# Expert activations made transposed, with the gates spread over the rank rows by a trip through DRAM

## The chip, the core and the metric

The kernel runs on one core of a Trainium2 chip. The metric is the device time of one execution in microseconds; before the change it is 426.72 us, the median of three runs (426.12 to 431.16).

## What is computed

An attention with spatially reduced keys, followed by a mixture of adapters. For each of 4 batches, 12288 queries of 128 channels attend to 768 keys, which are 4x4 means of `kv` times `w_sr` (keys and values are the same). Each of the 49152 results `x` is then routed to its best two of 8 experts, each a product of rank 16, and the gated sum is added to `x`:

```python
kv_pool = kv.reshape(B, H//4, 4, W//4, 4, C).mean(axis=(2, 4))
k = v = kv_pool.reshape(B, -1, C) @ w_sr
a = softmax(q @ k.T / sqrt(C));  x = (a @ v).reshape(B*N, C)
logits = x @ w_gate                      # 8 experts
w = softmax over the two largest logits  # 0 for the other six
out = x + sum_e w[:, e] * ((x @ A[e]) @ B[e])   # A: 128x16, B: 16x128
```

## The kernel before

The queries are cut into 96 chunks of 512 tokens (four sub-blocks `s` of 128). One round of the main loop (a step, loop variable `k`) issues the scores of chunk `k` and, woven between them by hand, the later stages of earlier chunks. Nearly everything keeps the order in which it is written (`keep`), on every engine's queue. The stages of one chunk:

- `scores` (L237): three pairs of matmuls `sg` (512 columns each) and three exponentials `em` on ScalarE. `sg` has two buffers in PSUM.
- `attend` (L247): 24 matmuls `acc`, six first and eighteen at the end of the step; one buffer in PSUM. `normalize` (L255): `rinv` and `xn` on VectorE, which also makes the logits of the experts.
- `top`, `route`, `gates` (L275 to L315): four `srt` on VectorE; then the gates of a whole group on GpSimd with a tanh on ScalarE. Groups have 1, 1, 2, then eighteen times 4, eight times 2 and four times 1 chunks (L268); `first` and `size` name them. The tensor `gw` holds the gates with tokens on the partitions.
- `transposes` (L317): four TensorE transposes of `xn` of one chunk, and in the same PSUM tile `tt_ps` four of `hg` of the chunk before it; one copy `tts` of both on VectorE (on ScalarE in the tail, the steps from 96 on, when there is nothing left to score).
- `down` (L341): four matmuls `h_ps`, with a sub-block of `xT` as weights and `a_bf` moving; the result has tokens on the partitions and expert and rank along the row. `gate` (L346): one VectorE multiplication of `h_ps` by `gw`, broadcast over the rank, gives `hg`.
- `up` (L355): four matmuls `d_ps` with a sub-block of `hgT` as weights. `finish` (L360): one VectorE addition `osb`, one store to `out` from the SP queue.

All PSUM tiles but `sg` and `acc` (that is `tt_ps`, `h_ps`, `d_ps`, and those of the key preparation) take turns in the two buffers of one pool (`mtile`, L70): a tile has to wait until the one but one before it has been read.

Which step a chunk enters at (its `transposes` of `xn` and its `down`) is counted out ahead in `enter` (L409 to L416): one step after its group is normalized (`late`), one chunk per step, in a few steps two (`two`). A chunk of a group of four enters six steps after its scores; the last chunk enters at step 97, and the loop ends two steps later.

The SP queue issues, in program order, the loads of `kv` for the next batch (two of 256 KB per step in steps 4 to 15 of each 24), every fourth step a transposing load `qT` (L84) of 512 KB made from a bf16 copy of `q`, which GpSimd's queue has cast from DRAM to DRAM (`cast_q`, L77), and the store of each chunk. GpSimd also adds up the `kv` rows of the next batch (L169) between the gates.

Of the kernel before, what the change touches and what calls it, by code (L numbers as in the profile page):

```python
# [11 lines left out]
BF16 = mybir.dt.bfloat16  # L12
U16 = mybir.dt.uint16
FP16 = mybir.dt.float16
AF = mybir.ActivationFunctionType
ALU = mybir.AluOpType
# [4 lines left out]
def kernel(  # L21
# [10 lines left out]
    nc = tc.nc  # L32
    P = 128
    B, N, C = q.tensor.shape
    E, RK = 8, 16
# [3 lines left out]
    T = 512  # L39
    S = T // P  # L40
    GC = 4
    GT = GC * T
# [7 lines left out]
    prep = ctx.enter_context(tc.tile_pool(name="prep", bufs=1))  # L50
    kvpool = ctx.enter_context(tc.tile_pool(name="kvpool", bufs=3))
    per_b = ctx.enter_context(tc.tile_pool(name="per_b", bufs=2))
    qpool = ctx.enter_context(tc.tile_pool(name="qpool", bufs=4))
    ppool = ctx.enter_context(tc.tile_pool(name="ppool", bufs=7))
    xpool = ctx.enter_context(tc.tile_pool(name="xpool", bufs=5))
    rpool = ctx.enter_context(tc.tile_pool(name="rpool", bufs=4))
    gpool = ctx.enter_context(tc.tile_pool(name="gpool", bufs=6))
    run = ctx.enter_context(tc.tile_pool(name="run", bufs=3))
    opool = ctx.enter_context(tc.tile_pool(name="opool", bufs=6))
    qdram = ctx.enter_context(tc.tile_pool(name="qdram", bufs=1, space=bass.MemoryType.DRAM))  # L60
    ps_s = ctx.enter_context(tc.tile_pool(name="ps_s", bufs=2, space=bass.MemoryType.PSUM))
    ps_a = ctx.enter_context(tc.tile_pool(name="ps_a", bufs=1, space=bass.MemoryType.PSUM))
# [4 lines left out]
    def mm(*a, **k):  # L67
        return keep(nc.tensor.matmul(*a, **k))  # L68

    def mtile(shape, dtype=FP32, name="mb"):  # L70
        return ps_m.tile(shape, dtype, tag="mb", name=name)
# [55 lines left out]
    for m in range(GC):  # L127
        load_q(1, m * S, m * S + S)
    b_f = const.tile([P, C], FP32)
    keep(nc.sync.dma_start(b_f, moe_B.rearrange("e r c -> (e r) c")))  # L130
    a_f = const.tile([P, P], FP32)
    keep(nc.sync.dma_start(a_f, moe_A.rearrange("e c r -> c e r")))

# [5 lines left out]
    make_identity(nc, id_f)  # L139
    id_bf = const.tile([P, P], BF16)  # L140
    nc.vector.tensor_copy(id_bf, id_f)
    wext = const.tile([P, VC], FP32)
    nc.vector.tensor_copy(wext[:, 0:C], w_sr_sb)
    wT_ps = mtile([P, C], name="wT_ps")
# [86 lines left out]


    em, acc, xn, xg, srt, gw = {}, {}, {}, {}, {}, {}
    tts, xT, hgT, hp, hg, dp = {}, {}, {}, {}, {}, {}
    R = J // 2

    def scores(k, r):  # L237
# [41 lines left out]
        for s in range(S):  # L279
            keep(nc.vector.max(srt[k0][:, m, s], xn[k][:, s, C:VC]))  # L280

    later = []

    def route(k0):
        n = size[k0] * S
# [23 lines left out]
    def gates(k0, n, eng, arg, mask):  # L309
        th = rpool.tile([P, GC * S, 8], FP32, tag="th", name="th")[:, 0:n]  # L310
        keep(nc.scalar.activation(th, arg, AF.Tanh, bias=0.0, scale=0.5))  # L311
        w = gpool.tile([P, GC * S, 8], FP32, tag="gw", name="gw")
        keep(eng.tensor_tensor(w[:, 0:n], th, mask, op=ALU.mult))  # L313
        keep(eng.tensor_tensor(w[:, 0:n], w[:, 0:n], mask, op=ALU.add))  # L314
        gw[k0] = w  # L315

    def transposes(kx, kh, tail):  # L317

# [21 lines left out]

    def down(k):  # L341
        hp[k] = mtile([P, S, P], name="h_ps")
        for s in range(S):
            mm(hp[k][:, s], xT[k][:, s], a_bf, start=(s == 0), stop=(s == S - 1))

    def gate(k):  # L346
        k0, m = first[k], k - first[k]
        hg[k] = run.tile([P, S, P], BF16, tag="hg", name="hg")
        keep(nc.vector.tensor_tensor(  # L349
            hg[k].rearrange("p s (e r) -> p (s e) r", e=E),  # L350
            hp[k].rearrange("p s (e r) -> p (s e) r", e=E),
            gw[k0][:, m * S:(m + 1) * S].rearrange("p s e -> p (s e)")
            .unsqueeze(2).broadcast_to([P, S * E, RK]), op=ALU.mult))

    def up(k):  # L355
        dp[k] = mtile([P, S, C], name="d_ps")
# [10 lines left out]
            d.pop(k, None)  # L367

    LA = 4

    for m in range(GC):
        turn_q(0, m, nc.scalar)
# [20 lines left out]
    for g in range(2, 4):  # L393
        cast_q(g)
    a_bf = const.tile([P, P], BF16)
    keep(nc.vector.tensor_scalar(a_bf, a_f, 0.5, None, op0=ALU.mult))
    b_bf = const.tile([P, C], BF16)
    keep(nc.vector.tensor_copy(b_bf, b_f))
    turn_q(1, 0, nc.scalar)
# [10 lines left out]
    e = 0  # L410
    for k in range(NCHUNK):
        done = normed[first[k] + size[k] - 1]
        late = k < NCHUNK - 2
        two = size[k] < GC and (k % 4 == 0 or k > NCHUNK - 4) and len(enter.get(e, [])) < 2
        e = max(e if two else e + 1, done + late)
        enter.setdefault(e, []).append(k)  # L416
    last = max(enter)

    sums, rest = [], []
    kh, ku = [], []  # L420
    for k in range(LA, last + 3):
        b, i = divmod(k, NB)
        ks = k < NCHUNK
        ka = att.get(k, [])
        kx = enter.get(k, [])
        if k % GC == 0:
            g = k // GC
            if 2 <= g + 1 < B * NG:
                load_qT(g + 1)
            if 4 <= g + 2 < B * NG and g + 2 not in q_bf:  # L430
                cast_q(g + 2)
        if b + 1 < B:
            if i == 4:
                sums, rest = prepare(b + 1, nc.gpsimd)
            if 4 <= i < 16:
                h, j = divmod(i - 4, 4)
                load_kv(b + 1, h, j, 0)
                load_kv(b + 1, h, j, 1)

        def after_norm(kn):  # L440
            top(kn)
            if kn == first[kn] + size[kn] - 1:
                route(first[kn])

        kn = [n for n in att.get(k - 1, []) if normed[n] == k]
        if k == LA:
            for s in range(S):
                attend(0, s)
            ka = []
        if ks:  # L450
            scores(k, 0)
        while later:
            later.pop(0)()
        for n in kn:
            normalize(n)
            if not ks:
                after_norm(n)
        pairs = [(kx[j] if j < len(kx) else None, kh[j] if j < len(kh) else None)
                 for j in range(max(len(kx), len(kh)))]
        for x_, h_ in pairs[:1]:  # L460
            transposes(x_, h_, not ks)
        if k + 1 in range(GC + 1, 2 * GC):
            turn_q(1, (k + 1) % GC, nc.scalar)
        if ks:
            scores(k, 1)
        for u_ in ku:
            up(u_)
            finish(u_)
        for a_ in ka[:-1]:
            for s in range(S):  # L470
                attend(a_, s)
            normalize(a_)
            after_norm(a_)
        if ka and len(ka) == 1:
            attend(ka[0], 0)
        if ks:
            for n in kn:
                after_norm(n)
            scores(k, 2)
        for x_ in kx[:1]:  # L480
            down(x_)
            gate(x_)
        if rest and i in (14, 15, 16, 18, 19, 20, 21, 22, 23):
            rest.pop(0)()
        for a_ in ka[-1:]:
            for s in range(1 if len(ka) == 1 else 0, S):
                attend(a_, s)
        for x_, h_ in pairs[1:]:
            transposes(x_, h_, not ks)
        for x_ in kx[1:]:  # L490
            down(x_)
            gate(x_)
        ku = kh
        if not ks:
            for u_ in ku:
                up(u_)
                finish(u_)
            ku = []
        kh = kx
        if b + 1 < B and 8 <= i < 20:  # L500
            h, j = divmod(i - 8, 4)
            for _ in range(3 if j == 3 else 2):
                if sums[h]:
                    sums[h].pop(0)()
# [30 lines left out]
```

## Time and profile before

The profiled execution took 426.38 us, of which the traced span is 424.5 us.

| DMA queue | packets | MB | time of its packets, share of 16 engines' span |
|---|---|---|---|
| hardware queue of SP | 87600 | 64.11 | 56.6% |
| software queue of POOL | 704 | 11.54 | 15.1% |

| group of the profile (by instruction) | count | mean ns |
|---|---|---|
| ACT `em` 128x1024 | 288 | 1023 |
| DVE `xn` 128x544 | 96 | 724 |
| DVE `hg` 128x512 | 96 | 689 |
| DVE `osb` 128x512 | 96 | 689 |
| DVE `tts` 128x1024, a few 128x512 | 95 | 673 |
| DVE `srt` (four a chunk) | 384 | 153 |
| POOL `kvr` addition 128x512 | 63 | 1268 |
| POOL `gw`, each of two | 27 | 406 and 409 |

| DMA issue | count | KB | median us to landing |
|---|---|---|---|
| `kvr` from `kv`, SP | 96 | 256 | 5.4 |
| `out` from `osb`, SP | 96 | 256 | 3.4 |
| `qbf` cast, POOL | 22 | 512 | 6.8 |
| `qT` from `qbf`, SP | 22 | 512 | 7.6 |

How to read it: the page lists each engine's busy time. A matmul's end is modelled and matmuls overlap, so the time from one matmul's start to the next one's is what it takes of the engine, and the 220 ns that the page gives a matmul of 128 columns is mostly latency. The chain of waits follows the work that ended last back to its releasers. The granted clock of TensorE is 1.00 in all 40 slices but the last two, which show 0.5.

### The profile page before, as it was taken

To read this page: it belongs to the slowest core of one execution; us is meant where nothing else is said; L and a number is where in the kernel's file an instruction comes from. 1 tells how busy PE (TensorE), PEld (TensorE's weight loads), DVE (VectorE), ACT (ScalarE), POOL (GpSimd) and SP (SyncE) were. 2 spreads that over 40 slices of the span, in tenths; PEclk is the share of its full clock that TensorE was granted. 3 is DMA by queue.
4 is the path that set the end of the run, shared out by engine and by line. 5 is a ranking of instruction groups with operands and counts; after the bars stand their busy time and mean duration, and the time that the engine had idled before them with its cause. 6 is when DMAs were issued, how large, how long until landed. Compare 5 with 4: busy or idle time off the path is not lost.

```text
span 424.5 us, 11379 instructions
## 1 busy us (share of the span) xinstructions
PE 386.0 (91%) x4515; PEld 309.8 (73%) x4589; DVE 327.4 (77%) x967; ACT 292.9 (69%) x336; POOL 162.5 (38%) x263
## 2 busy tenths in 40 slices
PE   4798899999999999999999999999999989999753
PEld 3566777787878878787888777777878877778642
DVE  2544778788988878779888878779888888888853
ACT  3378567676777777676788777677777776677522
POOL 0010357965320557964330467783231312222000
PEclk9999999999999999999999999999999999999955
DMA  8998857886558999965647999998574629442112
GB/s 287 382 241 242 148 179 186 291 152 150 125 125 166 294 215 271 309 165 124 148 128 168 270 208 229 209 255 206 133 168 126 147 79 151 134 116 76 51 51 100
DMA packets 88645, 76.44 MB, mean 180 GB/s; under 512 B 50480, under 2 KB 75312, under 8 KB 88112
## 3 DMA queue, kind: packets, MB, share of 16 engines
q1 hardware_dynamic: 87600, 64.11, 56.6%
q0 software_dynamic: 704, 11.54, 15.1%
q8 instruction: 36, 0.59, 0.6%
q14 instruction: 17, 0.14, 0.1%
q10 hardware_dynamic: 288, 0.07, 0.1%
HBM read 50.53 MB, written 36.70 MB: 205 GB/s over the span
## 4 chain that ended last, share of the span: by engine, by line
PE 73%; DVE 11%; POOL 5%; DMA 4%; ACT 4%; issue 2%; ACTq 0%; DVEq 0%; POOLq 0%
PE acc L68 30%; PE sg L68 20%; PE tt_ps L68 9%; PE h_ps L68 5%; PE d_ps L68 5%; DVE hg L349 3%; DMA kvr<-in_kv_dram 3%; ACT em L245 2%; POOL kvr L169 2%; DVE xn L262 2%; DVE osb L362 1%; DVE tts L335 1%; PE v_ps L68 1%; DMA qf<-in_q_dram 1%; DVE rinv L257 1%
## 5 line engine op out<-in xcount | busy, mean ns | idle before, releaser
L245 ACT ACTIVATE em<-sg 128x1024 f16<-128x1024 f32 x288 | 280.5, 1023 | 97.6 <-PE sg L68 67.4
L68 PE MATMUL acc<-vx,em 128*128 128x137 f16 x2304 | 174.7, 225 | 2.0 <-DVE xn L262 1.9
L68 PE MATMUL sg<-qT,kfT 128*128 128x512 bf16 x502 | 155.1, 379 | 2.7 <-ACT em L245 2.2
L68 PEld LDWEIGHTS <-em 128*128 128x128 f16 x2304 | 150.3, 98 | 4.9 <-DVE xn L262 2.2
L68 PEld LDWEIGHTS <-tts 128*128 128x128 bf16 x768 | 59.2, 99 | 53.1 <-ACT tts L333 5.6
L349 DVE TENSOR_TENSOR hg<-h_ps,gw 128x512 bf16<-128x512 f32 x96 | 66.1, 689 | 30.5 <-POOL gw L314 10.7
L292 POOL TENSOR_TENSOR over<-xn,srt 128x128 f32<-128x128 f32 (+1 forms) x54 | 19.7, 384 | 171.9 <-DVE srt L280 171.9
L169 POOL TENSOR_TENSOR kvr<-kvr 128x512 f32<-128x512 f32 x63 | 78.8, 1268 | 6.4 <-DMA kvr<-in_kv_dram 5.5
L262 DVE TENSOR_TENSOR xn<-acc,rinv 128x544 f32<-128x544 f32 x96 | 69.5, 724 | 3.3
L362 DVE TENSOR_TENSOR osb<-d_ps,xn 128x512 f32<-128x512 f32 x96 | 65.9, 689 | 2.7 <-PE d_ps L68 2.6
L335 DVE COPY tts<-tt_ps 128x1024 bf16<-128x1024 bf16 (+1 forms) x95 | 63.9, 673 | 2.4 <-PE tt_ps L68 2.4
L68 PEld LDWEIGHTS <-xn 128*128 128x128 bf16 x384 | 29.5, 99 | 28.7 <-issue 6.2
L68 PEld LDWEIGHTS <-kfT 128*128 128x128 bf16 x576 | 45.9, 97 | 6.0 <-issue 3.7
L68 PE MATMUL tt_ps<-id_bf,xn 128*128 128x128 bf16 x384 | 37.6, 221 | 7.9 <-DVE hg L349 5.0
L68 PE MATMUL h_ps<-a_bf,tts 128*128 128x128 bf16 x384 | 37.9, 222 | 7.4 <-ACT tts L333 3.9
L257 DVE RECIPROCAL rinv<-acc 128x4 f32<-128x4 f32 x96 | 17.4, 181 | 32.7 <-PE acc L68 32.1
L68 PE MATMUL d_ps<-b_bf,tts 128*128 128x128 bf16 x384 | 38.1, 224 | 3.6 <-DVE hg L349 1.0
L68 PE MATMUL tt_ps<-id_bf,hg 128*128 128x128 bf16 x384 | 38.2, 223 | 3.2 <-DVE hg L349 2.8
L280 DVE MAX8 srt<-xn 128x8 f32<-128x8 f32 x384 | 34.6, 153 | 0.2
L68 PEld LDWEIGHTS <-hg 128*128 128x128 bf16 x384 | 26.1, 100 | 4.2 <-DVE hg L349 3.7
L311 ACT ACTIVATE th<-over 128x128 f32<-128x128 f32 (+2 forms) x33 | 9.1, 276 | 15.5 <-DVE over L297 12.2
L313 POOL TENSOR_TENSOR gw<-th,over 128x128 f32<-128x128 f32 (+1 forms) x27 | 11.0, 406 | 21.5 <-ACT th L311 21.4
(49 smaller groups left out, 152.5 us busy)
## 6 DMA issues: line engine op xcount, KB each, us to landing
kvr<-in_kv_dram SPq DMA_DIRECT2D x96, 256.0 KB, 5.4
out_dram<-osb SPq DMA_DIRECT2D x96, 256.0 KB, 3.4
qbf<-in_q_dram POOLq DMA_DIRECT2D x22, 512.0 KB, 6.8
qf<-in_q_dram SPq DMA_DIRECT2D x1, 1024.0 KB, 5.2
qf<-in_q_dram SPq DMA_DIRECT2D x4, 256.0 KB, 5.4
qT<-qbf SPq DMA_TRANSPOSE x22, 7.6
w_sr_sb<-in_w_sr_dram ACTq DMA_DIRECT2D x1, 64.0 KB, 4.3
b_f<-in_moe_B_dram SPq DMA_DIRECT2D x1, 64.0 KB, 4.9
```

Of the source, the lines that this page charges most:

```text
L68: return keep(nc.tensor.matmul(*a, **k))
L169: keep(adder.tensor_tensor(u[:, lo:hi], u[:, lo:hi], v[:, lo:hi], op=ALU.add))
L245: keep(nc.scalar.activation(em[k][:, 2 * r:2 * r + 2], ps, AF.Exp, bias=0.0, scale=scale))
L257: keep(nc.vector.reciprocal(ri, acc[k][:, :, VC]))
L262: keep(nc.vector.tensor_tensor(x, acc[k][:, :, 0:VC], ri.unsqueeze(2).broadcast_to([P, S, VC]), op=ALU.mult))
L280: keep(nc.vector.max(srt[k0][:, m, s], xn[k][:, s, C:VC]))
L292: keep(eng.tensor_tensor(d, lg, so[:, :, i].unsqueeze(2).broadcast_to([P, n, 8]), op=ALU.subtract))
L311: keep(nc.scalar.activation(th, arg, AF.Tanh, bias=0.0, scale=0.5))
L313: keep(eng.tensor_tensor(w[:, 0:n], th, mask, op=ALU.mult))
L335: keep(nc.vector.tensor_copy(sb[:, lo:hi], ps[:, lo:hi]))
L349: keep(nc.vector.tensor_tensor(hg[k].rearrange("p s (e r) -> p (s e) r", e=E), hp[k].rearrange("p s (e r) -> p (s e) r", e=E), gw[k0][:, m ...
L362: keep(nc.vector.tensor_tensor(osb, dp[k], xn[k][:, :, 0:C], op=ALU.add))
```

## The change

For 24 groups (all eighteen of four and six of two: chunks 4 to 87, called turned below) `down` is one matmul with `a_bf` as weights and the 512 tokens of `xT` moving. Its result has expert and rank on the partitions and tokens along the row. `gate` multiplies it by `gx`, gates of the same layout, and gives `hgT` directly; the chunk no longer goes through the second half of `transposes`, and its `up` comes one step after its `down`.

`gx` is made once per group. GpSimd writes the gates as fp16 in the order expert, sub-block (`gh`); two steps after routing a TensorE transpose (`gT_ps`), a VectorE copy (`gT`) and a store of up to 32 KB to DRAM (`gt`) follow; one step after that a load reads each expert's row sixteen times, 512 KB for a group of four (`gx`). Rank and expert change places in `a_bf` and `b_f`, so that a partition is rank times 8 plus expert; `b_f` is loaded in eight pieces. The chunks of turned groups enter five steps after normalization and no longer one. Near the end two chunks enter in other steps than before. Of the buffers, `qpool` has 3 and no longer 4, `ppool` 6 and no longer 7, `xpool` 6 and no longer 5.

```diff
+    turned = {k0 for k0, n in size.items() if first[k0] == k0 and n > 1 and 4 <= k0 < NCHUNK - 8}
+    later, turns = [], []
...
     def gates(k0, n, eng, arg, mask):
         th = rpool.tile([P, GC * S, 8], FP32, tag="th", name="th")[:, 0:n]
         keep(nc.scalar.activation(th, arg, AF.Tanh, bias=0.0, scale=0.5))
+        if k0 in turned:
+            keep(eng.tensor_tensor(th, th, mask, op=ALU.mult))
+            gh[k0] = gpool.tile([P, P], FP16, tag="gh", name="gh")
+            keep(eng.tensor_tensor(gh[k0][:, 0:n * E].rearrange("p (e s) -> p s e", e=E),
+                                   th, mask, op=ALU.add))
+            turns.append([lambda: turn_gates(k0, n), lambda: spread_gates(k0, n)])
+            return
...
+    def turn_gates(k0, n):
+        ps = mtile([P, P], FP16, name="gT_ps")
+        mm(ps[0:n * E], gh[k0][:, 0:n * E], id_h, is_transpose=True, start=True, stop=True)
+        sb = gtpool.tile([P, P], FP16, tag="gT", name="gT")
+        keep(nc.vector.tensor_copy(sb[0:n * E], ps[0:n * E]))
+        gt[k0] = gdram.tile([P, P], FP16, tag="gt", name="gt")
+        keep(nc.sync.dma_start(gt[k0][0:n * E], sb[0:n * E]))
+
+    def spread_gates(k0, n):
+        gx[k0] = gxpool.tile([P, GT], FP16, tag="gx", name="gx")
+        src = gt[k0][0:n * E].rearrange("(e s) t -> e (s t)", e=E)
+        keep(nc.sync.dma_start(gx[k0][:, 0:n * P],
+                               src.unsqueeze(0).broadcast_to([RK, E, n * P])))
...
     def down(k):
         hp[k] = mtile([P, S, P], name="h_ps")
+        if first[k] in turned:
+            mm(hp[k], a_bf, xT[k], start=True, stop=True)
+            return
...
     def gate(k):
         k0, m = first[k], k - first[k]
+        if k0 in turned:
+            hgT[k] = run.tile([P, S, P], BF16, tag="hgT", name="hgT")
+            keep(nc.vector.tensor_tensor(
+                hgT[k], hp[k], gx[k0][:, m * T:(m + 1) * T].rearrange("p (s t) -> p s t", s=S),
+                op=ALU.mult))
+            return
...
     LA = 4
+    TURN = 5
...
-        late = k < NCHUNK - 2
-        two = size[k] < GC and (k % 4 == 0 or k > NCHUNK - 4) and len(enter.get(e, [])) < 2
+        late = TURN if first[k] in turned else k < NCHUNK - 2
+        two = len(enter.get(e, [])) < 2 and (
+            k < GC and k % 4 == 0 or k > NCHUNK - 24 and k % 3 == 0 or k > NCHUNK - 4)
...
         for x_, h_ in pairs[:1]:
             transposes(x_, h_, not ks)
+        for w in waiting:
+            w.pop(0)()
+        waiting = [w for w in waiting if w]
+        waiting += turns
+        turns.clear()
...
-        kh = kx
+        ku = ku + [x_ for x_ in kx if first[x_] in turned]
+        kh = [x_ for x_ in kx if first[x_] not in turned]
```

Counted out with the new `late` and `two`: the chunks of a group of four enter ten steps after their scores and no longer six; no chunk enters at steps 10 to 13 and 89; two enter at steps 84, 86, 88, 94, 96, 98 and 99 (before: 81, 84, 95 and 96); the last two enter at step 99 and no longer one at 97.

## The prediction

> **What bounds the kernel now.** I read the page first: busy times, then the chain that ended last.
>
> ```profile
> PE 386.0 (91%) x4515; PEld 309.8 (73%) x4589; DVE 327.4 (77%) x967; ACT 292.9 (69%) x336; POOL 162.5 (38%) x263
> ...
> PE 73%; DVE 11%; POOL 5%; DMA 4%; ACT 4%; issue 2%; ACTq 0%; DVEq 0%; POOLq 0%
> ```
>
> TensorE carries 73% of the chain, so the next view is the timeline of TensorE and ScalarE over one step, in a stretch where nothing is prepared for the next batch. Columns: start, us, engine, line, operation.
>
> ```profile
> 211.96 0.39 PE L68 MATMUL tt_ps<-id_bf,xn 128*128 128x128 bf16 x4
> 212.18 0.39 PE L68 MATMUL tt_ps<-id_bf,hg 128*128 128x128 bf16 x4
> 212.41 0.38 PE L68 MATMUL sg<-qT,kfT 128*128 128x512 bf16 x1
> 212.84 0.39 PE L68 MATMUL d_ps<-b_bf,tts 128*128 128x128 bf16 x4
> 213.06 0.54 PE L68 MATMUL acc<-vx,em 128*128 128x137 f16 x6
> 213.44 0.59 PE L68 MATMUL sg<-qT,kfT 128*128 128x512 bf16 x2
> 213.87 0.39 PE L68 MATMUL h_ps<-a_bf,tts 128*128 128x128 bf16 x4
> 214.09 1.28 PE L68 MATMUL acc<-vx,em 128*128 128x137 f16 x18
> ...
> 215.64 0.39 PE L68 MATMUL tt_ps<-id_bf,xn 128*128 128x128 bf16 x4
> ```
>
> ```profile
> 212.22 2.87 ACT L245 ACTIVATE em<-sg 128x1024 f16<-128x1024 f32 x3 [0.92 <-PE sg L68]
> ```
>
> Starts follow each other without a gap: a step is 215.64 - 211.96 = 3.68 us and TensorE issues all the time. Four 128-column matmuls take 0.22, a pair `sg` 0.43, the 24 `acc` 1.50. Most steps from 102 to 395 us last 3.68. Longer ones come beside key preparation:
>
> ```profile
> DVE hg L349 <- POOL gw L314: 10.7, 13, 1.8
> ```
>
> ```profile
> 191.77 0.38 PE L68 MATMUL tt_ps<-id_bf,xn 128*128 128x128 bf16 x4 [0.76 <-DVE hg L349]
> ```
>
> ```profile
> 350.12 0.38 PE L68 MATMUL d_ps<-b_bf,tts 128*128 128x128 bf16 x4 [0.43 <-DVE tts L335]
> ```
>
> The first (waits; total, times, longest) and second lines: GpSimd, busy with `kvr`, is late with a group's first gates. The third: where a step needs one PSUM tile more, `d_ps` waits until `tts` has been read out of its buffer. Last, the SP queue and the DMA share:
>
> ```profile
> 240.19 6.63 SPq L84 DMA_TRANSPOSE qT<-qbf  x1
> 246.91 2.18 SPq L95 DMA_DIRECT2D kvr<-in_kv_dram  x2
> 249.19 0.56 SPq L363 DMA_DIRECT2D out_dram<-osb  x1
> ```
>
> ```profile
> DMA to landing us min/median/max: 4.6/7.6/16.8
> ```
>
> ```profile
> 212.13:226.85 14.72, 14.56 (x185) 11.89 (x185) 12.64 (x37) 11.66 (x13) 3.22 (x7) 1.00 0.59 133
> 134.10:159.00 24.90, 24.19 (x301) 19.65 (x304) 19.96 (x60) 19.59 (x23) 11.31 (x18) 1.00 1.02 242
> 402.30:424.50 22.20, 10.37 (x84) 8.17 (x83) 10.37 (x33) 4.44 (x7) 0.00 (x0) 0.53 0.19 72
> ```
>
> The landing line is that of `qT`. In the stretches, the last three numbers are granted clock, DMA share and GB/s: DMA is 0.59 busy in a plain stretch and full while `kv` is loaded; the tail is a chain of waits (PE 10.4 of 22.2 us busy) at a clock of 0.53.
>
> **TensorE in a full step.** The four `tt_ps<-hg` go: 0.22. `down` keeps its 512 columns (4 x 0.055 against 0.215 for one `sg`): nothing. Then ScalarE is next: the third `sg` pair needs the buffer of the first, whose `em` ends at 212.22 + 1.02 = 213.24, so it can start at 213.29 (0.05 from a releaser to TensorE, as in every such row), and would now arrive at 213.22. So a step becomes 3.68 - 0.22 + 0.07 = 3.53. The `tts` copy halves to 0.42 (a 128x512 one at 343.05), VectorE from 3.4 to 3.1 a step; it was not the bound. Steps 14 to 94 are 81: 81 x 0.15 = **-12.2**. The gate's multiplication keeps its 0.69: same elements, PSUM still read.
>
> The Trainium skill (Perfetto Trace Analysis, Identifying the Most-Contended Engine) judges TensorE by its weight loads and the other engines by occupancy. By it VectorE, 77% against 73%, would be the engine to relieve, and the saving of 84 x (0.69 - 0.42) = 23 us on it would be the gain in place of my 12; the gapless starts above speak against that.
>
> **The turn.** `gT_ps` takes a PSUM buffer between `tt_ps` and `d_ps`, so `d_ps` of that step falls on the buffer of `tt_ps`, as at 350.12. `tts` starts at 212.61, ends at 213.03; `d_ps` starts at 213.08 where it would have started at 212.67 (0.06 for the turn itself included). Everything queued behind it on TensorE, the six `acc` and the third `sg`, moves with it; after the `em` wait it replaces, the step is 0.39 longer. Two of the 24 turns fall in empty steps: 22 x 0.39 = **+8.6**. Bounds: 0, if slack swallows it, and 0.43, the row. The copy `gT` (0.22, as a 128x128 cast) lies in VectorE's idle time.
>
> **Late gates.** The intervals from `xn` to `xn` that hold the nine waits of the second kind exceed their neighbours by 0.95 once and 1.33 twice per key preparation (186.93 to 192.18 is 5.25): 10.8. A turned group needs its gates only at the turn, about 1.9 us after the old `hg`; the longest wait was 1.8. What is left delays `sg` while `d_ps` waits anyway. **-10.8**. A strided `gh` that costs GpSimd more than 0.41 could give some of it back, 0.1 to 0.3 nine times.
>
> **Entries.** Five empty steps (10 to 13, 89) run like the sparse ones at 41 to 56 us (2.7 to 3.6), say 3.1: **-2.8**. Two double steps cost 2.5 each now (339.36 to 352.90 less three steps); four turned ones cost 0.67 of matmuls and about 1.0 of waits: **+1.8**. Steps 95 and 96, 10.17 us from 392.21 on because of a double with late gates, become ordinary: **-2.9**.
>
> **Tail.** It is a chain now: `tt_ps` 0.87, `tts` on ScalarE 1.0, `h_ps` 0.62, `hg` 0.70, the second chunk's copy 0.58 to 1.0, its `h_ps` and `hg`, then `osb` 0.69. Laid out with these rows and the two PSUM buffers, step 96 is 1.5 shorter (one chunk less in flight), 97 0.2 longer, 98 and 99 with two chunks each are new, 5.1 and 6.4, and the end is 0.7 longer: the last `osb` comes **+10.9** later. Bounds 7 (at full clock) to 13.
>
> **The gates' load.** SP's order per group: `gt` store ahead of `osb`, then `qT`, in `kv` stretches two `kvr`, then `gx`, which first waits for `gt` to land (stores land in 2.0 to 7 us; `qT` takes 2.1 to 6.6 to issue, which covers most of that). Behind `gx` wait the stores, with six `osb` buffers of slack. The gate that needs `gx` is three steps on, 10.4 us after the issue of `qT` (3.92 + 2 x 3.53, less 2.9 from `xn` to that issue, plus 2.3 from `xn` to the gate); 0.3 of lateness is free on VectorE, the rest stops `rinv`, hence `acc`. Cost of 512 KB in the queue: at least 1.4 (`kvr` of 256 KB are issued and land 0.68 apart at the start), at most 6.8 (the cast, same size, DRAM to DRAM). I take 1.4: same path as `kvr`. Then, with today's landings, `gx` comes at 6.6 to 11 us in most groups and at 11.8, 11.5, 13.5 and 20.4 behind the `qT` of 145.9, 161.8, 240.2 and 256.1: 1.1 + 0.8 + 2.8 + 9.7 = 14. The last stands on one `qT` that took 16.8 and may not recur: 5 without it. Each group also adds 1.7 to queues that are full in three stretches, up to 3 in each of them: at most +9. From 5 to 24, I take **+9**. At the start the seven further loads of `b_f` end by about 29 us; VectorE has 2.6 us idle there: 0.
>
> Sum: -12.2 + 8.6 - 10.8 - 2.8 + 1.8 - 2.9 + 10.9 + 9 = +1.6. Span 424.5 + 1.6 = 426.1; the profiled execution lies 1.9 above its span and 0.3 under the median, so 428.0 us.
>
> **Rivals.**
>
> 1. The gates are never late: without the +9 it is 419. For it: plain stretches with share 0.59. Against: share 1.02. Own range 414 to 424.
> 2. Slower: `gx` takes its time. All sixteen ranks read the same 32 KB, and no row shows such a read. Near the cast's 4.8 to 6.8 us in place of 1.4, it lands 7.6 + 4.8 = 12.4 after a median `qT`, 1.7 past the slack, in each of 24 groups, more where `kv` loads: 24 x 1.7 = 41 over 419 is 460, and stalls give the queue time back: 450. It decides from 3 us per load on.
> 3. The turn's wait does not show (its slack is found elsewhere) and gates are in time: 419 - 8.6 = 410.
>
> **Chances.** Forecast 0.37 (own range 423 to 436), rival 1 0.28, rival 2 0.25, rival 3 0.10. Two per cent, about what can be told from no change, is 418.2 to 435.3. Faster: rival 3 and 0.12 of rival 1, 0.22. Slower: rival 2 and 0.05 of the forecast, 0.30. Same 0.48. The range leaves out half of rival 3 and the upper half of rival 2: 414 to 448.
>
> **What would show it.** Full steps of 3.53 with TensorE waiting for `em`, or 3.46 without; `d_ps` waiting for `tts` once per group; no `tt_ps<-hg` waits at key preparation; VectorE's gate waiting for DMA `gx` behind `kv` loads alone (forecast), nowhere (1), or in every group (2); the stretch after the last `xn` but one of 33 us in place of 22. A `qT` or `qbf` that comes late by itself would break the sum.

## The result, and the profile after

| | median, us | lowest to highest | runs |
|---|---|---|---|
| before | 428.94 | 426.12 to 432.43 | 4 |
| changed | 456.21 | 451.53 to 460.05 | 4 |

The ratio is 1.054, 95% interval 1.038 to 1.070; it compares the runs that lie within 1.5% of the fastest one of their kernel, and so is not the ratio of these medians. The change is slower, where 428 had been forecast and 448 was the upper end of the range. The profiled execution took 451.53 us with a span of 449.7: 25.2 us more span than before, where the sum had said 1.6.

The page of the changed kernel: busy times, the chain by engine, and two groups.

```profile
PE 388.0 (86%) x3961; PEld 291.8 (65%) x4025; DVE 308.3 (69%) x987; ACT 297.8 (66%) x341; POOL 163.7 (36%) x263
...
PE 54%; DMA 19%; DVE 12%; POOL 4%; issue 4%; ACT 4%; SPq 2%; DVEq 0%; ACTq 0%
...
L381 DVE TENSOR_TENSOR hgT<-h_ps,gx 128x512 bf16<-128x512 f32 x84 | 58.0, 691 | 41.7 <-DMA gx<-gt 27.5
...
L322 POOL TENSOR_TENSOR gh<-th,over 128x128 f16<-128x128 f32 (+1 forms) x24 | 16.3, 678 | 1.9
```

TensorE has fewer instructions and yet a longer busy time, and its share of the chain has fallen from 73% to 54%, while DMA's has risen from 4% to 19%. The multiplication keeps its 0.69 us, but VectorE stood idle for 27.5 us ahead of it because `gx` had not landed. The timeline of TensorE over one plain step:

```profile
218.97 0.39 PE L71 MATMUL tt_ps<-id_bf,xn 128*128 128x128 bf16 x4
219.19 0.59 PE L71 MATMUL sg<-qT,kfT 128*128 128x512 bf16 x2
219.62 0.39 PE L71 MATMUL d_ps<-b_bf,hgT 128*128 128x128 bf16 x4
219.85 0.54 PE L71 MATMUL acc<-vx,em 128*128 128x137 f16 x6
220.30 0.38 PE L71 MATMUL sg<-qT,kfT 128*128 128x512 bf16 x1
...
222.50 0.39 PE L71 MATMUL tt_ps<-id_bf,xn 128*128 128x128 bf16 x4
```

222.50 - 218.97 is the 3.53 us of the forecast. The waits (total, times, longest) show what stands against it:

```profile
DVE hgT L381 <- DMA gx<-gt: 27.5, 12, 5.1
...
PE tt_ps L71 <- DVE hgT L381: 11.3, 4, 3.4
...
PE d_ps L71 <- DVE tts L363: 6.3, 16, 0.6
PE gT_ps L71 <- DVE hgT L381: 4.3, 2, 2.2
```

One late group, read on three engines. First SP's queue of issues:

```profile
131.61 0.33 SPq L337 DMA_DIRECT2D gt<-gT  x1
132.64 3.48 SPq L399 DMA_DIRECT2D out_dram<-osb  x1
136.22 2.14 SPq L87 DMA_TRANSPOSE qT<-qbf  x1
138.46 1.34 SPq L98 DMA_DIRECT2D kvr<-in_kv_dram  x2
139.89 0.56 SPq L342 DMA_DIRECT2D gx<-gt  x1
```

VectorE's multiplication that needs it, with the wait ahead of it:

```profile
146.62 0.69 DVE L381 TENSOR_TENSOR hgT<-h_ps,gx 128x512 bf16<-128x512 f32 x1 [3.22 <-DMA gx<-gt]
```

And TensorE from there on:

```profile
144.88 0.39 PE L71 MATMUL tt_ps<-id_bf,xn 128*128 128x128 bf16 x4
147.37 0.22 PE L71 MATMUL gT_ps<-id_h,gh 128*128 128x128 f16 x1 [2.10 <-DVE hgT L381]
...
148.54 0.38 PE L71 MATMUL d_ps<-b_bf,hgT 128*128 128x128 bf16 x4 [0.53 <-DVE tts L363]
148.76 0.77 PE L71 MATMUL acc<-vx,em 128*128 128x137 f16 x6
149.32 1.06 PE L71 MATMUL sg<-qT,kfT 128*128 128x512 bf16 x2
150.17 0.63 PE L71 MATMUL h_ps<-tts,a_bf 128*128 128x512 bf16 x1
```

The trip of a group's gates is store, landing, issue, landing. Here `gt` is issued at 131.61, lands at 136.84, `gx` is issued at 139.89 and lands at 146.53: 14.9 us. The multiplication was ready at 146.62 - 3.22 = 143.40, 11.8 us after the issue of `gt`. TensorE waits behind it, and then something follows that the sum had not held: `sg` takes 1.06 instead of 0.59 and `acc` 0.77 instead of 0.54. The stretches (from, to and length; busy times; then granted clock, DMA share, GB/s) say why:

```profile
145.50:148.90 3.40, 1.01 (x10) 0.60 (x10) 1.97 (x5) 1.51 (x2) 0.56 (x1) 1.00 1.41 382
148.90:152.30 3.40, 3.40 (x25) 2.58 (x23) 1.66 (x6) 1.20 (x2) 1.93 (x2) 0.50 0.67 234
416.21:449.70 33.49, 16.63 (x140) 13.02 (x140) 14.37 (x38) 8.23 (x12) 0.00 (x0) 0.59 0.17 63
```

After a stretch with 1.0 of 3.4 us of TensorE work the granted clock is 0.50 for 3.4 us. There are five such slow stretches between 60 and 300 us, four of 3.4 us and one of 6.8, where the kernel before had none ahead of 403. The third line is the tail, 33.5 us instead of 22.2.

Where the 25.2 us of span lie, step by step from one `xn` of VectorE to the next: start to `xn` of chunk 8 +0.4 (`a_f` lands late behind the other loads and VectorE waits 5.3 us for it, most of which is made good); chunks 8 to 11 -1.6; 12 to 78 +14.2; 79 to 93 +0.8; from chunk 94 on +11.3 (rounded, so that they add up to 25.1).

To price the lateness, each step of chunks 8 to 93 is compared with the shortest that the same step has in seven runs with this schedule (the changed kernel and the runs below that keep its steps, but for the first). The changed kernel has 28.6 us above that. 27.4 of it belong to `gx`: 19.7 in the steps that wait, 7.7 in the steps right behind them (5.50 instead of 3.88 us twice, 6.29, 5.65 and 5.70 instead of 4.38), which run at half clock. The sum, called "late" below, is used for the runs that keep the schedule. Seven of the nine steps that lose over 0.25 us to `gx` stand in the stretches with `kv` loads, the sign that the prediction named for its forecast.

### The profile page after: what moved, and what is told of

It is laid out like the page before. It is cut to its first block, busy times and chain, and to the rows that moved or that the text cites. A ratio compares the mean times of both kernels' runs of the same rounds, so it can differ in the third digit from the quotient of the medians.

```text
span 449.7 us, 10433 instructions
## 1 busy us (share of the span) xinstructions
PE 388.0 (86%) x3961; PEld 291.8 (65%) x4025; DVE 308.3 (69%) x987; ACT 297.8 (66%) x341; POOL 163.7 (36%) x263
## 3 DMA queue, kind: packets, MB, share of 16 engines
q0 software_dynamic: 704, 11.54, 14.7%
## 4 chain that ended last, share of the span: by engine, by line
PE 54%; DMA 19%; DVE 12%; POOL 4%; issue 4%; ACT 4%; SPq 2%; DVEq 0%; ACTq 0%
PE acc L71 21%; PE sg L71 15%; DMA gx<-gt 8%; DMA out_dram<-osb 8%; PE d_ps L71 5%; PE h_ps L71 5%; PE tt_ps L71 5%; DVE osb L398 3%; ACT em L251 2%; SPq L98 2%; DVE tts L363 2%; POOL kvr L175 2%; ACT tts L361 1%; DVE hgT L381 1%; DMA w_sr_sb<-in_w_sr_dram 1%
## 5 line engine op out<-in xcount | busy, mean ns | idle before, releaser
L251 ACT ACTIVATE em<-sg 128x1024 f16<-128x1024 f32 x288 | 281.6, 1024 | 110.4 <-PE sg L71 81.1
L71 PEld LDWEIGHTS <-em 128*128 128x128 f16 x2304 | 155.9, 100 | 20.4 <-DVE xn L268 5.0
L71 PE MATMUL sg<-qT,kfT 128*128 128x512 bf16 x512 | 159.3, 383 | 2.9 <-ACT em L251 2.2
L381 DVE TENSOR_TENSOR hgT<-h_ps,gx 128x512 bf16<-128x512 f32 x84 | 58.0, 691 | 41.7 <-DMA gx<-gt 27.5
L71 PE MATMUL tt_ps<-id_bf,xn 128*128 128x128 bf16 x384 | 38.3, 224 | 14.0 <-DVE hgT L381 11.3
L71 PEld LDWEIGHTS <-hgT 128*128 128x128 bf16 x336 | 25.9, 99 | 29.2 <-issue 12.9
L363 DVE COPY tts<-tt_ps 128x512 bf16<-128x512 bf16 (+1 forms) x90 | 38.0, 422 | 2.0 <-PE tt_ps L71 2.0
L71 PE MATMUL d_ps<-b_bf,hgT 128*128 128x128 bf16 x336 | 32.8, 222 | 6.8 <-DVE tts L363 6.3
L71 PE MATMUL h_ps<-tts,a_bf 128*128 128x512 bf16 x84 | 33.0, 393 | 4.5 <-DVE tts L363 2.8
L318 ACT ACTIVATE th<-over 128x128 f32<-128x128 f32 (+2 forms) x33 | 9.1, 275 | 13.8 <-DVE over L304 10.4
L71 PEld LDWEIGHTS <-tts 128*128 128x128 bf16 x96 | 8.1, 118 | 14.9 <-ACT tts L361 11.7
L361 ACT COPY tts<-tt_ps 128x1024 bf16<-128x1024 bf16 (+1 forms) x10 | 8.0, 796 | 14.6 <-PE tt_ps L71 14.6
L322 POOL TENSOR_TENSOR gh<-th,over 128x128 f16<-128x128 f32 (+1 forms) x24 | 16.3, 678 | 1.9
```

Source lines behind the costliest of these rows:

```text
L251: keep(nc.scalar.activation(em[k][:, 2 * r:2 * r + 2], ps, AF.Exp, bias=0.0, scale=scale))
L322: keep(eng.tensor_tensor(gh[k0][:, 0:n * E].rearrange("p (e s) -> p s e", e=E), th, mask, op=ALU.add))
L361: keep(nc.scalar.copy(sb[:, lo:hi], ps[:, lo:hi]))
L363: keep(nc.vector.tensor_copy(sb[:, lo:hi], ps[:, lo:hi]))
L381: keep(nc.vector.tensor_tensor(hgT[k], hp[k], gx[k0][:, m * T:(m + 1) * T].rearrange("p (s t) -> p s t", s=S), op=ALU.mult))
```

## The experiments

**1. The place in SP's queue.** `gx` is issued at the top of its step, ahead of `qT` and the two `kvr`:

```diff
         kx = enter.get(k, [])
+        for w in [w for w in waiting if len(w) == 1]:
+            waiting.remove(w)
+            w.pop()()
         if k % GC == 0:
...
         for w in waiting:
             w.pop(0)()
-        waiting = [w for w in waiting if w]
         waiting += turns
```

> The changed kernel with one thing moved: the load gx of a group is issued at the very top of its step, ahead of qT and of the two kvr loads, and no longer behind them. Nothing is left out. Theory (place in the queue): gx is late because it stands behind qT and kvr; it should now land within 7 us of its issue, some 3 us before its gate, VectorE's 27.5 us of waiting for gx and the half-clock stretches that follow should go, and the span should fall by about 27 to 423 us. Rival (the DMA engines are simply full while kv loads): what gx gains, qT, kvr or the stores lose; some other wait for DMA takes the place and the span stays over 435.

468.78 us, 1.082 of before, 1.068 to 1.096: worse still. SP's queue, in the profile of that run:

```profile
154.07 0.55 SPq L337 DMA_DIRECT2D gt<-gT  x1
154.71 0.38 SPq L399 DMA_DIRECT2D out_dram<-osb  x1
160.75 0.55 SPq L342 DMA_DIRECT2D gx<-gt  x1
161.41 4.00 SPq L87 DMA_TRANSPOSE qT<-qbf  x1
```

`gt` needs 6.7 us to land; now SP stands still for it, because the issue of `qT` no longer covers that time, and all that is queued behind waits too. SP waits for `gt` 23 times, 53.6 us in all, where the changed kernel has 3 times and 5.5 us. The trip itself is shorter here (6.3 to 12.5 us in the groups of four, 10.9 to 16.2 in the changed kernel), but in seven of these groups the store `gt` is issued 7 to 10 us late, behind such a wait. Standing behind `qT` and `kvr` was what covered the store's landing, so `gx` can't be helped by moving it forward in this queue; what the place alone costs, the run doesn't tell.

**2 and 3. Sixteen readers of one 32 KB block.** Both runs load `gx` from a bf16 copy of `q` (so the product is another one) and don't wait for `gt`. In the first each partition reads 4 KB of its own, in the second sixteen partitions read the same 4 KB, as the change does:

```diff
-        src = gt[k0][0:n * E].rearrange("(e s) t -> e (s t)", e=E)
+        src = q_bf[2].rearrange("(p j) c -> p (j c)", p=P)[:, 0:n * P]
...
-        src = gt[k0][0:n * E].rearrange("(e s) t -> e (s t)", e=E)
+        src = q_bf[2][0:P].rearrange("(e j) c -> e (j c)", e=E)[:, 0:n * P]
```

> The changed kernel, but gx is filled from 128 different rows of 4 KB (bf16 queries in DRAM, same bytes and same place in the queue) in place of 8 rows read 16 times each; the gates so applied are meaningless. gt is still stored, and nothing waits for it. Theory (a read of the same 32 KB by all sixteen engines is slow): the 4096-byte packets fall from 269 ns to about 170, gx lands 1.4 us behind the DMA before it and no longer 3.3 to 3.9, VectorE's wait for gx falls from 27.5 to about 10 us, the span to about 432. Rival (the rows do not matter, the load meets other traffic): packets and waits as in the changed kernel, span within 4 us of 449.7.

> The control of the run with different rows: gx is filled from 8 rows of 4 KB of the bf16 queries, read 16 times each as in the changed kernel; the gates so applied are meaningless, and nothing waits for gt. Both theories: as the changed kernel, packets near 269 ns, span within 4 us of 449.7. If it is faster by 5 us or more, the wait of the SP queue for gt to land was part of the lateness.

Own rows: 446.80 us, waits for `gx` 25.2, packets of 4 KB 252 ns, late 24.2. Shared rows: 450.74, 28.7, 299 ns, 29.6. The change itself: 27.5, 269 ns, 28.6. Sharing costs some 5 us at most, by one run of each; rival 2's mechanism, a slow read of the same rows, is refuted as the main cause. The landing of `gt` is not it either: the shared rows don't wait for it and are as late.

**4. The loads away.** The first `gx` serves all groups; the turns and the `gt` stores stay.

```diff
+        if k0 > 4:
+            gx[k0] = gx[4]
+            return
         gx[k0] = gxpool.tile([P, GT], FP16, tag="gx", name="gx")
```

> The changed kernel, but gx is loaded for the first turned group alone and all later groups use it (their gates are not applied); turns and stores of gt stay. It takes away 23 of 24 loads. Both theories: no wait for gx after the first group, no half-clock stretch before the tail, steps of 3.53 and 3.88 throughout, span 449.7 - 27 = 423 us. If more than 5 us above that, something else than the loads delays the main part.

433.43 us (two runs, 429.75 with the profile), span 427.9, late 8.3, of which 6.7 are two single events (that first load, and one `qT`). The clock is 0.50 once ahead of the tail, behind that `qT`, which neither theory had expected. So the loads cost some 22 us of span. Without the late steps the rest of the change stands at 427.9 - 8.3 = 419.6, 4.9 under the kernel before; the sum had -7.4 for it.

**5. Shorter packets.** The load of a group of four as two of 1024 columns, with rows of 2 KB:

```diff
-        keep(nc.sync.dma_start(gx[k0][:, 0:n * P],
-                               src.unsqueeze(0).broadcast_to([RK, E, n * P])))
+        for c in range(0, n * P, GT // 2):
+            keep(nc.sync.dma_start(gx[k0][:, c:c + GT // 2],
+                                   src[:, c:c + GT // 2].unsqueeze(0).broadcast_to([RK, E, GT // 2])))
```

> The spread load of a group of four is issued as two loads of 1024 columns, so its rows in DRAM and on the chip are 2 KB long instead of 4 KB. In the changed kernel the 4 KB packets took 269 ns each and the 2 KB ones 96 ns on average. If the length of the packets makes the load slow, the halves have packets of about 96 ns, both together take about 1.5 us in the queue, VectorE's waits for gx fall from 27.5 us to under 10, and the time falls from 451.5 to about 436 or less. If the bytes and the company in the queue make it, the new packets take about 135 ns, the waits stay within 5 us of 27.5, and the time is 446 to 457.

448.94 us (441.79 to 448.95), waits 26.4 us, late 26.6. From the first issue to the last landing the two halves take 5.6 us in the median, the whole load 6.3. The time is lower than the changed kernel's 451.5 to 460, which is of another series, but the waits are all but unchanged: the length of a packet is not the main cause.

**6. Two more steps of slack**, for groups of four alone:

```diff
-        late = TURN if first[k] in turned else k < NCHUNK - 2
+        late = TURN + (size[k] == GC) * 2 if first[k] in turned else k < NCHUNK - 2
```

> Chunks of turned groups of four enter seven steps after their group is done instead of five (groups of two stay at five; the last step stays 99, with two more empty steps at the start and two more double steps at the end). If the loads are merely late, two steps of 3.53 us cover the longest wait of 5.1 us: the waits for gx fall to under 5 us, no main step is at a granted clock of 0.5, and the span is 449.7 minus about 27 for the late steps plus 3 to 4 for the two doubles, about 426, a time near 428. If the queue is so full that a load issued earlier only ends later or pushes qT and kvr back, waits for gx or for qT of over 10 us remain and the time stays above 440.

> The kernel with seven steps between the gates and their use, once more with a profile. In its first profile the waits for gx were down from 27.5 us to 2.3, but one transposing load qT landed 27 us after its issue and TensorE waited 12.5 us for it; the span was 445.0, without that step's excess 430. If that landing is a chance event, this profile has no wait for qT of over 3 us and a span near 430. If the full stretches push the transposing loads back in each run, a qT wait of 5 us or more appears again and the span is above 437.

The waits for `gx` fall to 2.3 us and, in the second profile, to 4.0; the times stay at 439 to 449 in one series and 433 and 438 in the other, not at 428. In the first profile one `qT` lands 27 us after its issue and TensorE stands for 12.5 us; in the second no `qT` is late (13.8 us at most), but GpSimd waits 3.0 us for a `kvr` load and comes late to `gh`, TensorE waits 2.2 us for that, right after 2.2 us for `em` (ScalarE, too, had waited 3.1 us for GpSimd), and the clock in the next 8 us is 0.59. The lateness has moved to other loads of the same queues. That one `qT` was a single event; that something is late was not.

**7. Without the company.** The `kv` loads of later images and GpSimd's sums left out:

```diff
-                sums, rest = prepare(b + 1, nc.gpsimd)
-            if 4 <= i < 16:
-                h, j = divmod(i - 4, 4)
-                load_kv(b + 1, h, j, 0)
-                load_kv(b + 1, h, j, 1)
+                sums, rest = [[], [], []], prepare(b + 1, nc.gpsimd)[1]
+                for h in range(3):
+                    kvr[b + 1, h] = kvr[b, h]
```

> The changed kernel without the kv loads and without GpSimd's sums of images 2 to 4: their keys and values are made again from the first image's sums, so these outputs are another computation. Gates' stores and loads, the transposing loads and the casts stay. In the kernel before, the DMA engines are already busy 0.96 to 1.08 of the time in the stretches that hold the kv loads (158 to 186 us for one) and 0.5 to 0.7 outside. If the gates' load is late because it comes last in a full stretch, the waits for gx fall from 27.5 us to under 5 and the span to about 449.7 - 27 = 423 (some 2 less if GpSimd's gh also comes earlier). If the load is slow by itself, its 4 KB packets still take over 230 ns, waits of 15 us or more stay, and the span is above 435.

One run, 428.06 us: span 426.2, late 4.9, and among VectorE's waits:

```profile
DVE hgT L381 <- DMA gx<-gt: 8.4, 6, 2.1
```

That is between the two expectations, nearer to the first. Most of the lateness needs the `kv` loads beside it, or GpSimd's sums, which went with them; the 4 KB packets still take 282 ns. The trips now lie between 11.2 and 13.8 us, at or just over the slack; in the changed kernel between 10.9 and 16.2.

**8. A quarter of the bytes**, the first chunk's gates for all four, with five steps and with seven:

```diff
-        keep(nc.sync.dma_start(gx[k0][:, 0:n * P],
-                               src.unsqueeze(0).broadcast_to([RK, E, n * P])))
+        keep(nc.sync.dma_start(gx[k0][:, 0:T],
+                               src[:, 0:T].unsqueeze(0).broadcast_to([RK, E, T])))
...
-                hgT[k], hp[k], gx[k0][:, m * T:(m + 1) * T].rearrange("p (s t) -> p s t", s=S),
+                hgT[k], hp[k], gx[k0][:, 0:T].rearrange("p (s t) -> p s t", s=S),
```

> The changed kernel with a quarter of each gates' load: 512 columns (128 KB, rows of 1 KB) are loaded instead of 2048, and all four chunks of a group are multiplied by the first one's gates, so this is another computation; the order, the gt stores, the number of loads and the turns stay. If the price of the loads goes by their bytes in a full stretch, the waits for gx fall from 27.5 us to about a quarter or less (under 7) and the span from 449.7 to about 425 to 430. If it goes by the trip (the store, its landing, the issue, the landing of the load, each some microseconds however small), waits of 15 us or more stay and the span is above 438.

> Seven steps and, as in the run before it, a quarter of each gates' load, all four chunks of a group multiplied by the first one's gates (another computation). With both the trip and the bytes covered no wait for gx is left, and if the extra bytes are what pushes qT back, no wait for qT either: span about 428 to 430. If qT comes late without the bytes too, it is not the gates' load that does it: span above 435.

Five steps: 438.91 us (436.40 and 441.42), span 434.5, late 14.7, between the two expectations. VectorE's wait and the DMA issues (KB each, median us to landing):

```profile
DVE hgT L381 <- DMA gx<-gt: 16.3, 8, 3.7
```

```profile
gx<-gt SPq DMA_DIRECT2D x24, 128.0 KB, 3.4
gt<-gT SPq DMA_DIRECT2D x18, 32.0 KB, 4.1
```

The load of 512 KB took 6.3 from issue to landing; a quarter of it takes 3.4. So about half of the price (28.6 to 14.7) goes by the bytes. What stays is a trip of 8.8 to 13.9 us: 6.8 in the median from the issue of `gt` to that of `gx`, which stands behind `qT` and `kvr` (7.0 in the changed kernel), and then the landing. The landing of the store, 4.1 here, is not a further term: SP's queue covers it, and run 3, which doesn't wait for it, was as late.

Seven steps: 426.29 us with the profile (431.66 is the median of two), span 424.4, no wait for `gx`, one of 1.0 for `qT`. The stretch from 60 to 330 us in three kernels (last three numbers: clock, DMA share, GB/s), first the changed one, then seven steps with the whole load, then with a quarter:

```profile
60.00:330.00 270.00, 244.86 (x2558) 184.86 (x2599) 194.64 (x630) 191.74 (x213) 135.81 (x188) 0.96 0.88 215
```

```profile
60.00:330.00 270.00, 253.78 (x2697) 191.11 (x2741) 205.59 (x663) 204.05 (x226) 138.47 (x192) 0.98 0.99 223
```

```profile
60.00:330.00 270.00, 259.66 (x2809) 195.74 (x2854) 214.08 (x692) 212.02 (x235) 142.32 (x204) 1.00 0.90 205
```

And the kernel before:

```profile
60.00:330.00 270.00, 260.06 (x3170) 211.18 (x3222) 225.25 (x655) 201.38 (x224) 137.39 (x192) 1.00 0.81 193
```

With slack enough for the trip, the whole load fills the DMA engines to 0.99 and some load is late; a quarter leaves 0.90, and next to nothing is. Why the second, unprofiled run of that kernel took 437 stays open.

**9. Late gates alone.** The kernel before with one thing of the change: groups of four enter two steps late instead of one.

```diff
-        late = k < NCHUNK - 2
+        late = 2 if size[k] == GC and k > 3 else k < NCHUNK - 2
```

> The kernel before with one thing of the change alone: chunks of groups of four enter two steps after the group is done instead of one, nothing is turned. The step counts of the schedule: last step 97 as before, one more empty step and one more double step. If the late gates cost what the sum said (10.8 us for the nine steps that wait for hg and their neighbours), the time is 427 minus 10.8 plus about 1.7 for the double, 418. If TensorE's work only shifts, because the steps next to them are shorter already, it is above 424. Nothing should wait for gw any more.

418.59 us (418.15 to 420.25), 0.981 of before, 0.973 to 0.989; span 416.2. One of the steps in which `tt_ps` waited 0.76 us for `hg` before (the one that VectorE's `xn` of chunk 36 begins with), now:

```profile
165.13 0.39 PE L68 MATMUL tt_ps<-id_bf,xn 128*128 128x128 bf16 x4
165.36 0.39 PE L68 MATMUL tt_ps<-id_bf,hg 128*128 128x128 bf16 x4
```

Chunks 8 to 78 are 10.8 us shorter, 79 to 93 2.5 longer (one more double). This version beats both kernels, without anything turned.

**10. The price of a stall.** The kernel before, with VectorE's gate multiplication repeated at six chunks, no transfer involved:

```diff
     def gate(k):
...
-        keep(nc.vector.tensor_tensor(
+        for _ in range(1 + {18: 2, 22: 3, 42: 4, 46: 6, 66: 8, 74: 10}.get(k, 0)):
+            keep(nc.vector.tensor_tensor(
```

> The kernel before with VectorE's gate multiplication repeated 2, 3, 4, 6, 8 and 10 extra times (0.69 us each, the same result written again) at chunks 18, 22, 42, 46, 66 and 74, so that TensorE is held up for lengths that rise from about nothing to 6 us, with no transfer involved. If a hold-up of 2 us and more lowers the granted clock, the windows behind the longer ones show a clock of 0.5 for about 3.4 us, and the step of the hold-up or the next one is about 1.7 us longer than the hold-up itself explains. If the slow steps in the changed kernel came from the transfers, the clock stays above 0.9 here and each step is longer by the hold-up alone.

| repeats | TensorE waits, us | step (`xn` to `xn` on VectorE) longer by | next step longer by |
|---|---|---|---|
| 2 | 0.47 | 0.93 | -0.29 |
| 3 | 1.19 | 1.65 | -0.29 |
| 4 | 1.92 | 2.38 | -0.29 |
| 6 | 3.36 | 3.83 | 2.34 |
| 8 | 4.81 | 5.28 | 1.35 |
| 10 | 6.27 | 6.73 | 1.50 |

The stretches of the third and fourth (the step with the wait, then what follows):

```profile
213.75:219.81 6.06, 4.14 (x53) 3.26 (x52) 5.83 (x14) 3.89 (x4) 0.00 (x0) 1.00 0.65 147
219.81:223.49 3.68, 3.68 (x48) 2.97 (x49) 3.27 (x10) 2.07 (x3) 1.26 (x3) 1.00 0.19 71
230.55:238.06 7.51, 4.15 (x52) 3.25 (x51) 7.21 (x15) 3.89 (x4) 0.00 (x0) 0.91 0.70 190
238.06:241.50 3.44, 3.44 (x21) 2.33 (x22) 2.29 (x7) 1.06 (x2) 0.51 (x2) 0.50 0.63 195
```

Up to a wait of 1.9 us the step is longer by the wait and 0.46 and the next one shorter by 0.29, so that 0.17 is lost beyond the wait; from 3.4 on the clock is 0.50 behind it, and 1.8 to 2.8 us are lost beyond it. The slow steps come from the stall and not from the transfers. In the changed kernel waits of 2.1 us at `gT_ps`, followed by another 0.5 at `d_ps`, were enough.

The length of a single wait doesn't decide. In each trace all changes of the granted clock behind its first record lie on one grid of 3.41 us, so a slow stretch lasts 3.41 us or a multiple. Here are stretches of that grid: around the waits of 1.92 and 3.36 us of this run (the last line follows on the second), and around one of 1.50 and one of 0.53 us in the run with own rows (2):

```profile
216.28:219.70 3.42, 1.54 (x21) 1.13 (x18) 3.28 (x6) 1.63 (x2) 0.00 (x0) 1.00 0.63 170
233.35:236.76 3.41, 1.28 (x17) 0.87 (x14) 3.24 (x6) 1.37 (x2) 0.00 (x0) 1.00 0.86 197
236.76:240.18 3.42, 2.18 (x15) 1.64 (x16) 2.81 (x6) 0.68 (x1) 0.00 (x0) 0.50 0.83 262
```

```profile
140.29:143.70 3.41, 1.38 (x15) 0.86 (x14) 1.97 (x5) 1.91 (x2) 0.00 (x0) 1.00 1.44 422
143.70:147.12 3.42, 3.42 (x25) 2.58 (x23) 1.66 (x6) 1.16 (x2) 2.48 (x2) 0.50 0.67 208
```

With 1.54 us of TensorE work in a stretch (the first number behind its length) the next one stays at 1.00, as the 3.41 us from 219.70 on do; with 1.28, 1.38 or, in the changed kernel, 1.0 it gets 0.50. So what counts in these traces is how much work a stretch of the grid is left with, whether one wait takes it away or two.

**11. The turn's place.** The run with one load, with the turn moved behind `gate`:

```diff
-        for w in waiting:
-            w.pop(0)()
-        waiting = [w for w in waiting if w]
-        waiting += turns
-        turns.clear()
...
         for x_ in kx[:1]:
             down(x_)
             gate(x_)
+        for w in waiting:
+            w.pop(0)()
+        waiting = [w for w in waiting if w]
+        waiting += turns
+        turns.clear()
```

> As the run with one gates' load (later groups are not multiplied by their own gates; span 427.9), and the turn of the gates is put behind the step's down projection and gate instead of ahead of its second scores. There are 24 turns, of which each cost 0.36 us by the steps (3.89 against 3.53), with 0.2 to 0.9 us more where TensorE waited for GpSimd's gh. If the price is the wait of the up projection for tts behind the turn's copy, it falls to the turn's own transpose of about 0.1 us: span 427.9 - 24 x 0.3 - 2 = about 419. If the price is the work itself wherever it stands, the steps stay at 3.89 and the span at 426 to 429.

433.51 us (432.69 and 434.32), span 432.5, outside both expectations. In plain steps the turn costs 0.06 us instead of 0.36 (3.59 against 3.89), so the price is indeed the wait of `d_ps`. But nine turns stand in steps with key preparation, and there the next tile in the two buffers pays instead:

```profile
PE v_ps L71 <- DVE hgT L384: 4.3, 6, 0.7
```

Those steps are 0.6 longer, and the first load, issued later, makes two steps 5.8 us longer.

**12. Both together.** Groups up to chunk 63 turned, seven steps, the turn behind the gate, late gates for the other groups of four:

```diff
-    turned = {k0 for k0, n in size.items() if first[k0] == k0 and n > 1 and 4 <= k0 < NCHUNK - 8}
+    turned = {k0 for k0, n in size.items() if first[k0] == k0 and n > 1 and 4 <= k0 < 64}
...
-    TURN = 5
+    TURN = 7
...
-        late = TURN if first[k] in turned else k < NCHUNK - 2
+        late = TURN if first[k] in turned else 2 if size[k] == GC and k > 3 else k < NCHUNK - 2
...
-            k < GC and k % 4 == 0 or k > NCHUNK - 24 and k % 3 == 0 or k > NCHUNK - 4)
+            k < GC and k % 4 == 0 or k > 64 and k % 3 == 0 or k > NCHUNK - 4)
```

> The changed kernel with what the runs point to: groups up to chunk 63 alone are turned, they enter seven steps late, the turn stands behind the gate, the groups of four behind them enter two steps late, and one of three later chunks goes as a double, so that the last step is 97 again. From the 416.2 us span of the kernel before with late gates: about 55 full steps at 3.53 instead of 3.68 save 8.3, five more empty steps save 1.9, five more doubles cost 9.5, some 20 turns cost 0.1 each: 417 to 418 if no load is late, a time of 419 to 420, so that it does not beat the 418.6 of that kernel. If qT or gx are still late in the stretches with kv loads, it is 425 to 440.

432.82 us (426.62 to 435.19), 1.015 of before, 1.010 to 1.020. In the profiled run, the quickest of the five, `gx` is late once, by 1.3 us, and the span is 424.8, 7 over the expectation: the turns beside key preparation cost 0.6 to 0.7 each as in 11, and eight doubles of chunks that aren't turned take 9.2 to 9.9 us for two steps.

## Why the prediction was wrong

Right, by its own steps:

- **The full step.** 3.53 forecast and measured; the third `sg` starts some 0.07 after the sixth `acc` has been issued, so `em` is the next limit as said.
- **The turn.** 0.39 forecast, 0.35 measured (3.88 against 3.53), by the named wait; run 11 removes it in plain steps.
- **Late gates.** -10.8 forecast, -10.8 measured alone in run 9, 0.4 of it from the additional empty step.
- **Doubles and tail.** A turned double was put at 1.7 (0.67 and about 1.0) and costs 1.9 (5.24 + 4.11 us for two steps, against 3.53 + 3.88); the fourth one shows below, under steps 95 and 96. The tail: +10.9 forecast, +11.3 measured.

Wrong:

- **The gates' load**, +9 (bounds 5 to 24), measured 27.4: 18.4 of the 23.6 us that the sum was short. It stood on "I take 1.4: same path as `kvr`" and on a gate due 10.4 us after the issue of `qT`. Measured from that issue, the load lands after 7.8 to 14.6 us, and in 13 of the 18 groups of four after more than 10.3, where "6.6 to 11 in most groups" was forecast; and the gate was due after 7.2 to 12.0, because SP itself reached `qT` late (at 136.22 behind an `out` store that held the queue for 3.48). The 1.4 came from the start, where the `kvr` loads have the DMA engines all but to themselves:

```profile
10.00:20.00 10.00, 7.75 (x44) 5.11 (x45) 5.24 (x9) 3.41 (x5) 0.00 (x0) 1.00 1.09 382
```

The engines are full there and move 382 GB/s; in the `kv` stretch of the prediction they are as full, 1.02, and move 242. In the loop `gx` lands 1.4 to 5.0 us after the load ahead of it in the groups of four, 3.1 in the median (3.9 after the `kvr` at 142.65 in the group above). The row to price it by was there. That the issue of `qT` covers the landing of `gt`, as the prediction said, held: SP waits for it 3 times, 5.5 us in all.
- **What a stall costs.** The term for the load had only waits. 7.7 of the 27.4 us are the half clock behind them (run 10). The tail's line, with a clock of 0.53 beside 10.4 of 22.2 us busy, showed that a waiting TensorE loses its clock, and the sum used it for the tail alone. The Trainium skill (TensorE: Matmul & The Clock Gate, What's actually happening) says that the clock is halved after an idle window of about 3.4 us, free-running. The traces agree on the length, 3.41 us, and on the free running, the grid. They differ on what is idle: here a window with 1.38 us of work was followed by the half clock (shown under run 10), and the measurement decides.
- **Steps 95 and 96**, -2.9, measured +0.4: the schedule puts a double into step 94, whose second chunk falls there. **Empty steps**, -2.8, measured -0.7: 3.31 instead of 3.1, and 4.16 once where the turn waits 1.1 for GpSimd's `gh`, whose strided fp16 write takes 744 ns for 128x128, where `gw` in fp32 takes 454 (678 and 409 are means over two shapes). **Start**, 0, measured +0.4. The prediction's last step is also off by 0.3: 426.1 plus 1.9 plus 0.3 is 428.3 and not 428.0.

Rival 2 had the time nearly right, 450, and the condition too (a load that takes over 3 us), but by a mechanism that runs 2 and 3 refute as the main one: near by luck. About half of the lateness goes by the bytes of the load (run 8), and most of it needs the stretches with `kv` loads (run 7). The other half stays with a quarter of the bytes: there are `gx`'s place in SP's order, 7 us behind `gt`, and a landing of 3 us and more. How these two share that half stays open. The Trainium skill (DMA: Bandwidth & Descriptors, Anatomy of one DMA — SWDGE (gpsimd) path) says that a transfer issued from GpSimd has a fixed part of about 2 us, whatever its size. The transfers here are issued from SP: 128 KB took 3.4 us, and the 32 KB store 3.8 in the median and 1.4 at the least.

## What to carry to other kernels

Price a new transfer in the stretch in which it will run, from issue to landing, with each hop counted, and compare that trip with the time from its first issue to its first use; the spacing of loads that have the DMA engines to themselves doesn't hold where others run beside them. A stall of TensorE can cost more than its length: here, where waits left it 1.4 us of work or less in 3.41, the work behind ran at half clock. When a change bundles several edits, run the cheapest alone: here one step more between the gates and their use brought 8 us of span by itself, and the turned layout, which frees TensorE of 0.22 in 3.68 us, never earned its loads.

## What the runs showed of the hardware

- The granted clock of TensorE changes on a grid of 3.41 us. A stretch of it with 1.0 to 1.38 us of TensorE work was followed by one at 0.50, one with 1.54 by 1.00. So two waits of 1.50 and 0.53 us in one stretch brought the half clock, and one of 1.92 didn't.
- The 4 KB packets of the load took 252 to 301 ns in the mean of a run, whatever they read; the 2 KB ones of all loads 92 to 106. Halving the packets shortened the load from 6.3 to 5.6 us.
- Full DMA engines (share 1.0 to 1.1) moved 382 GB/s with `kvr` loads all but alone, and 242 with transposing loads, casts and stores beside them.
- A 128x128 fp16 write with a stride on GpSimd took 744 ns, the fp32 one without it 454.
